# Attention and a two-layer MLP: split weight blocks of the first group stored in DRAM and read back by the second

## The chip, the cores and the metric

One core of a Trainium2 chip runs the whole program. The metric is the device time of one execution in microseconds; three executions of the kernel before gave 865.79, 866.02 and 866.52 us, a median of 866.02 us.

## The reference

Four batches, twelve heads, 448 positions, head size 64. The inputs q and k are scaled up (by 6.845 and 6.865), all is computed to float32 accuracy.

```python
scores = scale * np.matmul(q, k.transpose(0, 1, 3, 2))        # causal mask, softmax
attn_out = np.matmul(softmax(scores), v)                      # (4, 12, 448, 64)
x = attn_out.transpose(0, 2, 1, 3).reshape(4, 448, 768)
u = x + (x.transpose(0, 2, 1) @ U @ V).transpose(0, 2, 1)     # low rank mix of positions
out = u + np.maximum(u @ w_ch1, 0.0) @ w_ch2                  # 768 -> 3072 -> 768
```

The two weights w_ch1 and w_ch2 arrive as float64 words, which the kernel decodes to float32 itself.

## The kernel before

The matmuls of the MLP take their operands in a rounded form, fp32r. To keep float32 accuracy each operand is split into a high part (the value rounded, a cast) and a low part (value minus high part), and each product is made of three matmuls: high by high, high by low, low by high.

**First group.** After most of the attention (some 200 us of the profile; its remains are mixed in for a while) batches 0 and 1 go through the MLP in the ordinary way (`mlp`, L452). The weights come in 48 blocks of 128 x 768 values (`blocks`, L404): for each of eight steps p over the hidden width, three blocks of w_ch1 (columns of the hidden layer) and three of w_ch2. A block is loaded as words (`load_w`), decoded on ACT, DVE and POOL (`decode_w`, `decode_bit`, `decode_sum`), stored in DRAM as float32 (`kept`, L420) for the second group, and split into high and low parts in one of two slots of the SBUF tile `wsp`: the cast on ACT, the subtraction on DVE (`split`, L197; in its early pieces `weight_piece`). `decode_ahead` does this one to four blocks ahead of the one that TensorE is on: at the first quarter of block n the split of block n+1, at the second the decoding of n+2, at the fourth the store of n+2 and the load of n+4.

**Second group.** Batches 2 and 3 go through the same MLP by Strassen's method in Winograd's form (`strassen`, L871): a *quad* is a 2 x 2 arrangement of weight pieces t0, t1, t2, t3, and seven products take the place of eight. There are 12 quads of w_ch1 (kind 1, pieces of 128 x 384, 63 matmuls each) and 18 of w_ch2 (kind 2, pieces of 128 x 256, 42 matmuls each), 1512 matmuls in all. The seven weight operands of a quad are t0 and t1 (group "A1"), three sums of pieces (group "S": `S23` and `S1`), and t1 minus a sum, which is written over t2, and t3 (group "A2"). So t0, t1 and t3 are used as they are, t2 only in sums.

`load_quad` (L593) reads a quad's float32 pieces from `kept` into a ring in the tile `wld` (two DMAs for kind 1, L605; four for kind 2, L612). `prepare` (L622) then makes the high and low parts of each group in a ring in `wsp`: the cast on ACT (L634), the subtraction through the helper `adder` (L511) on the engine that `WE = "PVVP"` (L73) names, which is POOL for A1 and A2 and DVE for S. The sums are made on DVE in tiles `sw`. Nothing here has due times: at each product `strassen` issues the next load if its ring has room (`load_next`), up to two groups if theirs has (`prepare_next`), and one round of steps of each group in work (`emit`). Each engine, and the queue of SyncE (SP) that issues all DMAs, works in the order in which the program was written down, and waits in place.

The products accumulate in PSUM banks `sa`, `sb` and `se`. Between products that share a bank, DVE adds the bank to its place (`adder` into `xb` or `r`), or ACT copies it (L718) or applies the ReLU (L715) (`results`, L708). Between kind 1 and kind 2, `hidden` (L742) makes the split sums of the hidden layer (`h`, `tmp`): casts on ACT (L519) and subtractions on DVE (L511). In the last step p the results are stored from SP as they come (`stored`, L829). The helper's line L511 thus stands for many operations, and tiles tell them apart.

Of the kernel before, what the change touches and what calls it, by code (L numbers as in the profile page):

```python
# [10 lines left out]
F32 = mybir.dt.float32  # L11
# [4 lines left out]
ALU = mybir.AluOpType  # L16

B, H, S, D = 4, 12, 448, 64
DM, DFF, R = 768, 3072, 32
P = 128  # L20
# [3 lines left out]
NC = DM // P  # L24
FS = 8
FC = DFF // P // FS
WB = NC * P
# [45 lines left out]
WE = "PVVP"  # L73
# [5 lines left out]
def attention_mix_mlp(ctx: ExitStack, tc: tile.TileContext, qk, v, w1, w2, vu, out):  # L79
# [6 lines left out]
    nc = tc.nc  # L86

    def pool(name, bufs, **kw):
        return ctx.enter_context(tc.tile_pool(name=name, bufs=bufs, **kw))
# [3 lines left out]
    dram = pool("dram", 1, space=bass.MemoryType.DRAM)  # L93


    wsp = main.tile([P, WSP], F32R, tag="wsp", name="wsp")
# [31 lines left out]
    def f(ap):  # L128
        return ap.bitcast(F32)

    st = {}
# [24 lines left out]
    def decode_bit(t, n, piece, a=None):  # L156

        lo, hi = t[:, :n, 0], t[:, :n, 1]
        if piece == 0:
            st["nwa"] = st.get("nwa", -1) + 1  # L160
            a = main.tile([P, WB], U32, tag=f"wa{st['nwa'] % 2}", name="wa")[:, :n]
            nc.scalar.activation(f(a), f(hi), AF.Abs)
        elif piece == 1:
            nc.vector.tensor_scalar(f(a), f(a), HI_MIN, HI_MAX, op0=ALU.max, op1=ALU.min)
        elif piece == 2:
            nc.vector.tensor_scalar(a, a, 3, 0x3FFFFFF8, op0=ALU.logical_shift_left, op1=ALU.bitwise_and)
        elif piece == 3:
            nc.vector.scalar_tensor_tensor(hi, hi, 0xC0000000, a, op0=ALU.bitwise_and, op1=ALU.bitwise_or)  # L168
        else:
            nc.scalar.activation(lo.bitcast(I32), lo, AF.Copy, scale=2.0**-29)  # L170
        return a

    def decode_bits(t, n):
        a = None
        for piece in range(5):
            a = decode_bit(t, n, piece, a)
        return a

    def decode_sum(t, a, n):
        nc.gpsimd.tensor_tensor(  # L180
            a.bitcast(I32), t[:, :n, 1].bitcast(I32), t[:, :n, 0].bitcast(I32), op=ALU.add
        )
# [14 lines left out]
    def split(src, hi, lo):  # L197
        nc.scalar.copy(hi, src)  # L198
        nc.vector.tensor_tensor(lo, src, f(hi), op=ALU.subtract)  # L199
# [204 lines left out]
    blocks = []  # L404
    for p in range(FS):
        blocks += [w1[p, k] for k in range(FC)] + [w2[p, k] for k in range(NC // 2)]
    kept = [dram.tile([P, WB], F32, name=f"kept{n}") for n in range(len(blocks))]

    def load_w(n):
        if n < len(blocks):  # L410
            st["wr", n] = load_words(blocks[n], WB)

    def decode_w(n, step):
        if n >= len(blocks):
            return
        if step == 0:
            st["wa", n] = decode_bits(st["wr", n], WB)
        elif step == 1:
            decode_sum(st.pop(("wr", n)), st["wa", n], WB)
            nc.sync.dma_start(out=kept[n], in_=f(st["wa", n]))  # L420
        else:
            o = NC * 2 * S + n % 2 * 2 * WB
            wh, wl = wsp[:, o : o + WB], wsp[:, o + WB : o + 2 * WB]
            split(f(st.pop(("wa", n))), wh, wl)
            st["w", n] = wh, wl

    def weight_piece(n, piece):
        if piece == 0:
            load_w(n)
        elif piece < 6:  # L430
            st["wa", n] = decode_bit(st["wr", n], WB, piece - 1, st.get(("wa", n)))
        elif piece == 6:
            decode_w(n, 1)
        else:
            o = NC * 2 * S + n % 2 * 2 * WB
            wh, wl = wsp[:, o : o + WB], wsp[:, o + WB : o + 2 * WB]
            st["w", n] = wh, wl
            if piece == 7:
                nc.scalar.copy(wh, f(st["wa", n]))
            else:  # L440
                nc.vector.tensor_tensor(wl, f(st.pop(("wa", n))), f(wh), op=ALU.subtract)

    def decode_ahead(blk, quarter):
        if quarter == 0:
            decode_w(blk + 1, 2)
        elif quarter == 1:
            decode_w(blk + 2, 0)
        elif quarter == 3:
            decode_w(blk + 2, 1)
            load_w(blk + 4)  # L450
# [59 lines left out]
    def adder(o, a, b, op=ALU.add, e="V"):  # L510
        (nc.vector if e == "V" else nc.gpsimd).tensor_tensor(o, a, b, op=op)  # L511
# [48 lines left out]
    NQ = 2  # L560
# [29 lines left out]
    used = set()  # L590
# [31 lines left out]
    def prepare(q, group, at):  # L622

        kind, _, _ = q
        w = NC // 2 * P if kind == 1 else NQ * P
        t = st["t", q]

        for key, n in {"A1": (("A1", 2),), "S": (("S23", 2), ("S1", 1)), "A2": (("A2", 2),)}[group]:
            r = wsp[:, at : at + 2 * n * w].rearrange("p (l i w) -> p l i w", l=2, i=n)
            st["ws", q, key] = r[:, 0], r[:, 1]  # L630
            at += 2 * n * w

        def hi(key, src):
            return lambda: nc.scalar.copy(st["ws", q, key][0], src())  # L634

        def lo(key, e, src):
            def step():
                h, l = st["ws", q, key]
                adder(l, src(), f(h), ALU.subtract, e)
                used.add((q, key, "ready"))  # L640

            return step

        if group == "A1":
            return [[hi("A1", lambda: t[:, 0:2])], [lo("A1", WE[0], lambda: t[:, 0:2])]]
        if group == "A2":

            def end():
                used.add((q, "split"))

            return [[hi("A2", lambda: t[:, 2:4])], [lo("A2", WE[3], lambda: t[:, 2:4]), end]]
        s = {}

        def s13():
            st["sums"] = True
            s[0] = main.tile([P, WB], F32, tag="wa0", name="sw")[:, :w]
            s[1] = main.tile([P, WB], F32, tag="wa1", name="sw")[:, : 2 * w]
            s[1] = s[1].rearrange("p (i w) -> p i w", i=2)
            adder(s[0], t[:, 2], t[:, 3])
            adder(s[1][:, 1], t[:, 0], t[:, 2], ALU.subtract)  # L660

        def s2():
            adder(s[1][:, 0], s[0], t[:, 0], ALU.subtract)

        def s4():
            adder(t[:, 2], t[:, 1], s[1][:, 0], ALU.subtract)
            used.add((q, "s4"))

        return [
            [s13],  # L670
            [s2, s4],
            [hi("S23", lambda: s[1])],
            [hi("S1", lambda: s[0]), lo("S23", WE[1], lambda: s[1])],
            [lo("S1", WE[2], lambda: s[0]), lambda: st.pop("sums")],
        ]
# [7 lines left out]

    def product(q, n, ms):
        (key, i), j, bank = PRODUCTS[n]
        h, l = st["ws", q, key]
        steps = []
        for m in ms:
            if q[0] == 1:
                bh, bl = (u[:, j] for u in uc[m])  # L690
            else:
                bh, bl = st["H", q[1], m][j]
            cs = slice(m * P, (m + 1) * P)
            steps += [(h[:, i, cs], bh), (h[:, i, cs], bl), (l[:, i, cs], bh)]
        end = ms[-1] == (NC // 2 if q[0] == 1 else NQ) - 1
        for k, (a, b) in enumerate(steps):
            nc.tensor.matmul(  # L697
                st[bank, q], a, b,
                start=(n in FIRST and ms[0] == 0 and k == 0),
                stop=(n in LAST and end and k == len(steps) - 1),  # L700
                skip_group_check=True,
            )
# [137 lines left out]
    def prepare_next():  # L840

        if prepared[0] == len(units):
            return
        q, group = units[prepared[0]]
        if group == "A2" and (q, "s4") not in used:
            return
        if ("t", q) not in st or group == "S" and st.get("sums"):
            return
        w = NC // 2 * P if q[0] == 1 else NQ * P
        at = wsp_ring.take(2 * GROUPS[group] * w, (q, group))  # L850
        if at is None:
            return
        prepared[0] += 1
        prep.append(prepare(q, group, at))
# [54 lines left out]
    def attention():  # L909
# [12 lines left out]
        for of, at in EARLY.items():  # L922
            for piece, (n, slot) in enumerate(at):
                step = (low_rank_weights, (piece,)) if of == "vu" else (weight_piece, (of, piece))
                early.setdefault((n, slot), []).append(step)
# [24 lines left out]
    with tc.manual_schedule():  # L950
        constants()
        todo = attention()
        while todo[0][0] < len(pairs):
            _, step, a = todo.pop(0)
# [6 lines left out]
        for i, _ in enumerate(mlp()):  # L961
            while done < len(todo) and done * DRAIN < len(todo) * (i + 1):
                _, step, a = todo[done]
# [64 lines left out]
```

## Time and profile before

| | |
|---|---|
| median of three executions | 866.02 us |
| the profiled execution | 866.12 us, of which the span from first to last instruction 864.3 us |
| TensorE matmuls busy (PE) | 849.6 us (98%) |
| VectorE busy (DVE) | 687.5 us (80%) |
| ScalarE busy (ACT) | 461.2 us (53%) |
| GpSimd busy (POOL) | 309.4 us (36%) |
| DMA | 98.98 MB, 34.3% of the 16 engines' span |
| granted TensorE clock | 1.00 |

An engine's busy time is the union of its instructions' spans. Matmuls overlap: one over 448 columns is shown with some 366 ns, but the next starts sooner, so the busy share of TensorE hides short gaps, and its pace is read from the distance of starts. "[0.87 <-ACT r L718]" behind an instruction says that its engine sat idle for 0.87 us before it, and which instruction released it.

### The profile page before, as it was taken

The page shows a single profiled execution, that of the slowest core. Times are in us where ns is not written, and L with a number is a line of the kernel's source. Part 1 is how long each engine was busy: PE and PEld are TensorE (multiplying, and loading weights), DVE is VectorE, ACT ScalarE, POOL GpSimd, SP SyncE. Part 2 cuts the span into 40 slices and gives each one's busy share as a digit, 9 for nine tenths or more (in the row PEclk, how much of TensorE's full clock was granted, in tenths as well). Part 3 has the DMA queues.
Part 4 walks back from the last instruction along what each step waited for, and adds up shares of the span by engine and source line. Part 5 has one row for each costly group of instructions (what it writes and reads, how often), then busy time and mean ns, then how long its engine had stood idle before and what let it go on. Part 6 is the DMA issues. An engine that isn't in the chain of part 4 may idle for free.

```text
span 864.3 us, 13588 instructions
## 1 busy us (share of the span) xinstructions
PE 849.6 (98%) x4728; PEld 752.0 (87%) x4728; DVE 687.5 (80%) x1392; ACT 461.2 (53%) x978; POOL 309.4 (36%) x342
## 2 busy tenths in 40 slices
PE   7999999999999999999999999999999999999998
PEld 5777777789989999999999999889998998899886
DVE  6988888957667676767776768798998989898896
ACT  6998988854342444453445353463544635445520
POOL 4655777832212222213222323223333333333330
PEclk9999999999999999999999999999999999999999
DMA  6243343214344344444444457321121122212103
GB/s 206 98 147 119 112 134 97 69 60 158 122 161 149 125 165 165 165 165 165 165 165 165 165 165 264 96 60 50 43 80 49 61 61 61 70 41 74 38 1 128
DMA packets 47060, 98.98 MB, mean 115 GB/s; under 512 B 4240, under 2 KB 25744, under 8 KB 46992
## 3 DMA queue, kind: packets, MB, share of 16 engines
q1 hardware_dynamic: 46992, 98.12, 34.3%
q8 instruction: 37, 0.61, 0.3%
q14 instruction: 31, 0.25, 0.1%
HBM read 73.73 MB, written 24.38 MB: 114 GB/s over the span
## 4 chain that ended last, share of the span: by engine, by line
PE 87%; DVE 9%; ACT 2%; issue 2%; DMA 1%; DVEq 0%; ACTq 0%
PE hf L465 20%; PE of L490 20%; PE sa L697 15%; PE se L697 7%; PE s L244 6%; PE pv L313 6%; PE t L297 5%; PE sb L697 4%; DVE h L511 2%; DVE sw L511 2%; DVE tmp L511 1%; PE y L362 1%; PE xt L345 1%; DVE wsp L511 1%; DVE xb L511 1%
## 5 line engine op out<-in xcount | busy, mean ns | idle before, releaser
L511 POOL TENSOR_TENSOR wsp<-wld,wsp 128x512 fp32r<-128x512 f32 (+1 forms) x60 | 105.9, 1773 | 215.3 <-ACT wsp L634 127.6
L490 PE MATMUL of<-g,wsp 128*128 128x448 f32 x864 | 177.7, 366 | 0.0
L490 PEld LDWEIGHTS of<-g,wsp 128*128 128x128 f32 x864 | 162.1, 188 | 12.6
L180 POOL TENSOR_TENSOR wa<-wld 128x768 int32<-128x768 int32 (+1 forms) x49 | 73.0, 1489 | 261.9 <-DVE wld L168 190.9
L286 POOL TENSOR_SCALAR p<-p,r 112x112 f32<-112x112 f32 (+1 forms) x192 | 94.1, 507 | 61.6 <-DVE r L281 25.1
L273 ACT ACTIVATE p<-p,m 112x112 f32<-112x112 f32 x192 | 99.7, 525 | 13.6 <-DVE m L259 13.6
L198 ACT CAST wsp<-wa 128x768 fp32r<-128x768 f32 x47 | 39.3, 837 | 117.3 <-POOL wa L180 117.3
L697 PE MATMUL sa<-h,wsp 128*128 128x448 f32 x432 | 98.8, 368 | 1.9 <-DVE xb L511 1.9
L465 PE MATMUL hf<-wsp 128*128 128x448 f32 x432 | 92.8, 367 | 0.0
L465 PE MATMUL hf<-u,wsp 128*128 128x448 f32 x432 | 92.3, 366 | 0.0
L697 PE MATMUL sa<-uch,wsp 128*128 128x448 f32 x288 | 89.5, 371 | 2.8 <-ACT r L718 2.8
L259 DVE CUSTOM_DVE_ANT_0 p<-s,mask 112x112 f32<-112x112 f32 (+1 forms) x192 | 74.6, 442 | 20.9 <-PE s L244 19.4
L697 PEld LDWEIGHTS sa<-h,wsp 128*128 128x128 f32 x432 | 80.7, 188 | 10.7 <-DVE xb L511 3.8
L493 DVE TENSOR_TENSOR xa<-of,xa 128x448 f32<-128x448 f32 x96 | 59.3, 621 | 35.5 <-PE of L490 34.9
L465 PEld LDWEIGHTS hf<-u,wsp 128*128 128x128 f32 x432 | 81.0, 188 | 6.5
L465 PEld LDWEIGHTS hf<-wsp 128*128 128x128 f32 x432 | 80.8, 188 | 6.2
L199 DVE TENSOR_TENSOR wsp<-wa,wsp 128x768 fp32r<-128x768 f32 x47 | 50.9, 1084 | 22.8 <-ACT wsp L198 22.5
L473 ACT ACTIVATE g<-hf 128x448 fp32r<-128x448 f32 x48 | 26.1, 545 | 79.0 <-PE hf L465 79.0
L474 DVE SCALAR_TENSOR_TENSOR g<-hf,g 128x448 fp32r<-128x448 f32 x48 | 29.9, 624 | 43.7 <-ACT g L473 43.6
L634 ACT CAST wsp<-sw 128x256 fp32r<-128x256 f32 (+3 forms) x60 | 33.9, 575 | 56.6 <-DVE sw L511 25.7
L697 PEld LDWEIGHTS sa<-uch,wsp 128*128 128x128 f32 x288 | 54.1, 188 | 10.9 <-ACT r L718 6.0
L634 ACT CAST wsp<-wld 128x512 fp32r<-128x512 f32 (+1 forms) x60 | 41.8, 703 | 38.1 <-PE sa L697 28.6
(95 smaller groups left out, 1619.0 us busy)
## 6 DMA issues: line engine op xcount, KB each, us to landing
wld<-in_w_dram SPq DMA_DIRECT2D x48, 768.0 KB, 4.6
kept<-wa SPq DMA_DIRECT2D x48, 384.0 KB, 2.6
qk<-in_qk_dram SPq DMA_DIRECT2D x24, 448.0 KB, 3.8
wld<-kept SPq DMA_DIRECT2D x24, 384.0 KB, 3.2
wld<-kept SPq DMA_DIRECT2D x72, 128.0 KB, 2.4
v<-in_v_dram SPq DMA_DIRECT2D x24, 224.0 KB, 2.8
out_dram<-xa SPq DMA_DIRECT2D x12, 224.0 KB, 2.5
out_dram<-xb SPq DMA_DIRECT2D x12, 224.0 KB, 1.9
```

Source lines behind the costliest of these rows:

```text
L180: nc.gpsimd.tensor_tensor(a.bitcast(I32), t[:, :n, 1].bitcast(I32), t[:, :n, 0].bitcast(I32), op=ALU.add)
L244: nc.tensor.matmul(o, t[r, 0, i * CP : (i + 1) * CP], t[r, 1, :n], start=True, stop=True, skip_group_check=True,)
L259: nc.vector.tensor_tensor_reduce(out=st["p", b, h][:, POFF[i] : POFF[i] + n], in0=st.pop(("o", b, h, i)), in1=mask[:, S - n :], scale=-(D* ...
L273: nc.scalar.activation(pi, pi, AF.Exp, bias=m[:, i : i + 1], scale=-1.0, accum_out=l[:, i : i + 1])
L286: nc.gpsimd.tensor_scalar(pi, pi, r[:, i : i + 1], 1.0, op0=ALU.mult, op1=ALU.mult)
L313: nc.tensor.matmul(o[j * D : (j + 1) * D, kt * CP : S], v[:, kt, j, :], pt[:, n0 : n0 + S - kt * CP], start=j not in begun, stop=not left[ ...
L465: nc.tensor.matmul(o, a[:, cs], m, start=(kc + n == 0), stop=(kc + n == NC + 1))
L490: nc.tensor.matmul(o, a[:, cs], m, start=(fc + n == 0), stop=(fc + n == FC + 1))
L493: nc.vector.tensor_tensor(x, o, x, op=ALU.add)
L511: (nc.vector if e == "V" else nc.gpsimd).tensor_tensor(o, a, b, op=op)
L634: return lambda: nc.scalar.copy(st["ws", q, key][0], src())
L697: nc.tensor.matmul(st[bank, q], a, b, start=(n in FIRST and ms[0] == 0 and k == 0), stop=(n in LAST and end and k == len(steps) - 1), skip ...
```

## The change

The first group also stores the high and low parts of each block in DRAM (`kept_s`, by `keep_split`, from SP, right behind the split). It stores only what the second group uses: of a block of w_ch1 in the second half of the hidden width the second half of its columns, of a block of w_ch2 in the first half the even ones of its 128-column pieces, of all others everything. In the second group, group A1 becomes one step on SP that reads both pieces' parts into `wsp` (two DMAs for kind 1, four for kind 2), with no cast and no subtraction. Group A2 reads the parts of t3 (one DMA for kind 1, two for kind 2), and casts and subtracts only t2, on ACT and POOL as before. Group S, `load_quad` and the products stay.

```diff
+    kept_s = [dram.tile([P, 2, WB], F32, name=f"halves{n}") for n in range(len(blocks))]
+
+    def keep_split(n):
+        p, k = divmod(n, FC + NC // 2)
+        o = NC * 2 * S + n % 2 * 2 * WB
+        src = f(wsp[:, o : o + 2 * WB]).rearrange("p (l c) -> p l c", l=2)
+        dst = kept_s[n]
+        if k < FC and p >= FS // 2:
+            src, dst = src[:, :, WB // 2 :], dst[:, :, WB // 2 :]
+        elif k >= FC and p < FS // 2:
+            src, dst = (
+                t.rearrange("p l (f d c) -> p l f d c", d=2, c=P)[:, :, :, 0] for t in (src, dst)
+            )
+        nc.sync.dma_start(out=dst, in_=src)
...
             split(f(st.pop(("wa", n))), wh, wl)
             st["w", n] = wh, wl
+            keep_split(n)
...
                 nc.vector.tensor_tensor(wl, f(st.pop(("wa", n))), f(wh), op=ALU.subtract)
+                keep_split(n)
...
+        def kept_parts(key, i, j):
+            _, p, k = q
+            dst = st["ws", q, key][2][:, :, i]
+            if kind == 1:
+                n = p * NQ + k + j // 2 * DFF // P // 2
+                src = kept_s[n // FC * (FC + NC // 2) + n % FC]
+                nc.sync.dma_start(out=dst, in_=src[:, :, j % 2 * w : (j % 2 + 1) * w])
+                return
+            for m in range(NQ):
+                n = p * NQ + m + j % 2 * DFF // P // 2
+                src = kept_s[n // FC * (FC + NC // 2) + FC + k]
+                c = n % FC * 2 * P + j // 2 * P
+                nc.sync.dma_start(out=dst[:, :, m * P : (m + 1) * P], in_=src[:, :, c : c + P])
+
         if group == "A1":
-            return [[hi("A1", lambda: t[:, 0:2])], [lo("A1", WE[0], lambda: t[:, 0:2])]]
+
+            def load():
+                for i in range(2):
+                    kept_parts("A1", i, i)
+                used.add((q, "A1", "ready"))
+
+            return [[load]]
         if group == "A2":
-
-            def end():
+            part = lambda: t[:, 2]
+
+            def hi2():
+                kept_parts("A2", 1, 3)
+                nc.scalar.copy(st["ws", q, "A2"][0][:, 0], part())
+
+            def lo2():
+                h, l, _ = st["ws", q, "A2"]
+                adder(l[:, 0], part(), f(h[:, 0]), ALU.subtract, WE[3])
+                used.add((q, "A2", "ready"))
                 used.add((q, "split"))
 
-            return [[hi("A2", lambda: t[:, 2:4])], [lo("A2", WE[3], lambda: t[:, 2:4]), end]]
+            return [[hi2], [lo2]]
```

## Rows read from the trace of the kernel before

**Rows 1.** Busy time by stage: the first group's MLP, then the second group.
```profile
core 0: us, PE busy (x) PEld busy (x) DVE busy (x) ACT busy (x) POOL busy (x), PEclk, DMA share, GB/s
203.00:541.00 338.00, 338.00 (x1690) 312.60 (x1689) 240.38 (x344) 144.75 (x199) 87.62 (x56) 1.00 0.48 164
541.00:865.00 324.00, 314.13 (x1515) 282.60 (x1513) 282.77 (x423) 147.31 (x247) 100.08 (x58) 1.00 0.20 61
```

**Rows 2.** PE's waits in the second group: us in total, times, longest.
```profile
PE sa L697 <- ACT r L718: 2.8, 6, 0.9
PE sa L697 <- DVE xb L511: 1.9, 3, 0.9
PE sb L697 <- DVE xa L493: 0.6, 1, 0.6
PE se L697 <- DVE r L511: 0.2, 1, 0.2
```

**Rows 3.** Timeline of PE: first and last product of the second group (start, us).
```profile
541.38 0.37 PE L697 MATMUL sa<-uch,wsp 128*128 128x448 f32 x1
...
859.31 1.50 PE L697 MATMUL sa<-h,wsp 128*128 128x448 f32 x6 [0.72 <-DVE xb L511]
```

**Rows 4.** Chain that ended last, second group: one undisturbed piece (start, us, what).
```profile
615.59 5.54 PE sa L697 x27
```

**Rows 5.** POOL by form, second group: busy us, mean ns | idle before.
```profile
L511 POOL TENSOR_TENSOR wsp<-wld,wsp 128x512 fp32r<-128x512 f32 x36 | 56.3, 1572 | 110.7 <-ACT wsp L634 72.2 <-issue 9.6 <-DVE wsp L511 8.7
L511 POOL TENSOR_TENSOR wsp<-wld,wsp 128x768 fp32r<-128x768 f32 x22 | 46.0, 2094 | 97.1 <-ACT wsp L634 47.9 <-PE sa L697 14.2 <-PE sb L697 13.6
```

**Rows 6.** DVE by form, second group, three subtractions of the hidden layer.
```profile
L511 DVE TENSOR_TENSOR h<-tmp,h 128x896 fp32r<-128x896 f32 x24 | 33.7, 1406 | 3.4 <-ACT h L519 3.4
...
L511 DVE TENSOR_TENSOR tmp<-r,tmp 128x448 f32<-128x448 f32 x24 | 22.0, 916 | 0.5
...
L511 DVE TENSOR_TENSOR h<-r,h 128x448 fp32r<-128x448 f32 x12 | 11.9, 989 | 3.3 <-ACT h L519 3.2
```

**Rows 7.** Tile tmp in the second group: duration ns min/median/max.
```profile
L511 DVE TENSOR_TENSOR h<-tmp,h x24: 1073/1092/2750, 560.8 to 834.1; 128x896 fp32r<-128x896 f32 x24
L511 DVE TENSOR_TENSOR tmp<-r,tmp x24: 608/624/1739, 561.9 to 832.4; 128x448 f32<-128x448 f32 x24
```

**Rows 8.** Timeline around the longest stop, four engines.
```profile
720.47 0.47 PE L697 MATMUL sa<-uch,wsp 128*128 128x448 f32 x1 [0.87 <-ACT r L718]
...
718.95 0.62 ACT L634 CAST wsp<-wld 128x512 fp32r<-128x512 f32 x1
...
719.79 1.70 DVE L511 TENSOR_TENSOR h<-r,h 128x448 fp32r<-128x448 f32 x1
...
719.65 1.35 POOL L511 TENSOR_TENSOR wsp<-wld,wsp 128x512 fp32r<-128x512 f32 x1 [6.54 <-ACT wsp L634]
```

**Rows 9.** The page's slices: GB/s of DMA in 40 equal slices.
```profile
GB/s 206 98 147 119 112 134 97 69 60 158 122 161 149 125 165 165 165 165 165 165 165 165 165 165 264 96 60 50 43 80 49 61 61 61 70 41 74 38 1 128
```

**Rows 10.** The page's DMA issues: count, KB each, us to landing.
```profile
wld<-in_w_dram SPq DMA_DIRECT2D x48, 768.0 KB, 4.6
...
wld<-kept SPq DMA_DIRECT2D x24, 384.0 KB, 3.2
wld<-kept SPq DMA_DIRECT2D x72, 128.0 KB, 2.4
```

**Rows 11.** Line L612: time of one issue on SP, ns min/median/max.
```profile
L612 SPq DMA_DIRECT2D wld<-kept x72: 359/460/497, 536.0 to 807.0; - x72
```

**Rows 12.** SP's waits in the second group.
```profile
SPq L612 <- POOL wsp L511: 75.7, 14, 11.0
SPq L605 <- POOL wsp L511: 75.5, 13, 15.9
```

**Rows 13.** Timeline: two POOL subtractions and the PE pieces with their first use.
```profile
589.43 1.61 POOL L511 TENSOR_TENSOR wsp<-wld,wsp 128x512 fp32r<-128x512 f32 x1
...
598.11 0.57 PE L697 MATMUL sa<-h,wsp 128*128 128x448 f32 x2
...
769.94 2.81 POOL L511 TENSOR_TENSOR wsp<-wld,wsp 128x768 fp32r<-128x768 f32 x1 [3.78 <-PE sa L697]
...
777.09 0.79 PE L697 MATMUL sa<-uch,wsp 128*128 128x448 f32 x2
```

More of the change, by code (lines that the diff above doesn't have):

```diff
@@ L629, in prepare @@
             r = wsp[:, at : at + 2 * n * w].rearrange("p (l i w) -> p l i w", l=2, i=n)
-            st["ws", q, key] = r[:, 0], r[:, 1]
+            st["ws", q, key] = r[:, 0], r[:, 1], f(r)
             at += 2 * n * w
@@ L637, in step @@
             def step():
-                h, l = st["ws", q, key]
+                h, l, _ = st["ws", q, key]
                 adder(l, src(), f(h), ALU.subtract, e)
@@ L685, in product @@
         (key, i), j, bank = PRODUCTS[n]
-        h, l = st["ws", q, key]
+        h, l, _ = st["ws", q, key]
         steps = []
```

## The prediction

> **What bounds the kernel now.** I read the stages first [rows 1]. TensorE is the bound in both groups. In the first group's MLP it is busy for all 338.00 us, so nothing can be won there and the question is only what the new stores may cost. In the second group 314.13 of 324 us are busy, while DVE has 282.77 us of work, nearly as much; POOL and ACT have far less.
>
> Next the waits of PE in the second group [rows 2]: eleven, 5.5 us of idle time. None is for a weight. In each, PE stands before a PSUM bank that ACT (copy, L718) or DVE (add, L511 and L493) has not emptied yet. Idle time understates the loss, because a matmul is shown longer than the distance to the next. The full loss comes from the pace: an undisturbed piece does 27 matmuls in 5.54 us [rows 4], 0.2052 us each, so 1512 need 310.2 us. The stage takes 859.31 + 1.50 - 541.38 = 319.4 us [rows 3]. The stops thus cost 9.2 us. The last one, 0.72 us before 859.31 [rows 3], is the end of the dependence chain itself (two last products share a bank, nothing else is left to do); with the restart I put it at 1.0 us and leave it. So 8.2 us can go at most.
>
> Why are ACT and DVE late? The longest stop shows it [rows 8]. PE waits until 720.47 for an ACT copy. Among the casts that ACT did just in front of it is one of a group A1 (0.62 us). Beside it DVE runs a subtraction over 448 columns in 1.70 us, where the shortest of that size takes 0.608 us [rows 7]. A POOL subtraction, the low part of a weight group, started 0.14 us before it and ended at 721.00, and the DVE operation ended at 721.49: DVE stood still until POOL was through. This is no single case. Three kinds of subtraction of the hidden layer have means of 1406, 916 and 989 ns [rows 6] against shortest ones of 1073, 608 and 608 [rows 7]: 24 x 0.333 + 24 x 0.308 + 12 x 0.381 = 20.0 us of DVE time in the second group that is only standing beside POOL. The sums of weight pieces show the same and I leave them uncounted.
>
> **The change part by part.**
>
> *POOL in the second group.* 58 subtractions take 102.3 us there [rows 5] (two more run just before). The 30 of A1 go, the 30 of A2 halve: about 18 x 0.79 + 12 x 1.05 = 26.8 us stay, a quarter. With it a quarter of the 20.0 us of DVE's standing stays, 5 us, and 15 us leave DVE. POOL itself is on no path; its own gain is worth nothing.
>
> *ACT in the second group.* 30 casts go and 30 halve. A cast of A1 takes 0.62 us [rows 8] or somewhat more, and stands in front of the copies that PE waits for; some 25 to 30 us leave an engine with 147.31 us [rows 1].
>
> *What that gives PE.* Both engines that PE waits for get work taken out from just in front of the late operations. An average stop is 8.2/10 = 0.8 us; one clash that is avoided brings DVE forward by 1.70 - 0.61 = 1.1 us [rows 7, 8], and an avoided cast ACT by 0.6 us. So where a clash or cast stood before the stop, the stop goes whole. Bounds: none goes if DVE's own work is the cause (0), all go (-8.2 us). I take the share of POOL's work that disappears, three quarters, because the stretched operations stand near most of the stops: -6.1 us. What is late next is the last hidden layer, where DVE has a dense run of such subtractions with little POOL work beside it.
>
> *New loads in the second group.* 12 x 3 + 18 x 6 = 144 DMAs, 12 x 3 x 384 + 18 x 6 x 128 KB = 28.3 MB, over 319 us 89 GB/s more beside 61 [rows 1]. All are issued by SP, in order. An A1 load waits for its place in the ring (PE done with what lay there), as the cast did; behind it on SP queue the next `load_quad`, the other groups' loads and at the end the stores of the results. Before, from free place to ready took a cast and a subtraction, 0.62 + 1.57 = 2.2 us [rows 5, 8]. Now, for kind 2, four issues of 0.46 us [rows 11] and a landing of 2.4 us [rows 10]: 4.2 us; kind 1 two issues and 3.2 us, about the same. So the weights come 2 us later. Pairing the 60 POOL subtractions with the first product that uses each, in program order, the shortest distance of an A1 is 598.31 (the second matmul of the piece at 598.11) minus 591.04 = 7.3 us, the shortest of an A2 777.41 - 772.75 = 4.7 us [rows 13]; in that A2 the new load needs one issue and 3.2 us against the old subtraction's 2.81 us. The work that hides it is that distance, PE on the products before. Cost between 0 and, if a few of the tightest ones slip by 2 us each, 4 us; I take +0.5, since the rows lie nearer to the lower end.
>
> *New stores in the first group.* 48 stores, 24 of 768 KB and 24 of 384 KB, again 28.3 MB: 84 GB/s on top of 164 at a share of 0.48 [rows 1], so about 248 GB/s and a share of 0.73. The 25th slice already moves 264 GB/s [rows 9] inside the stretch in which PE never stops. A store waits on SP for DVE's low part; behind it stand the float32 store and the load of the words of a block that is decoded more than one block (7 us) later, against a landing of 4.6 us [rows 10]. The slot in `wsp` that a store reads is written again two blocks later, 14 us. Cost 0; if that cover were gone, one landing, 4.6 us, paid once and then carried along.
>
> No row shows compute beside DMA at a share of 0.73. The Trainium skill, "SBUF — State Buffer", section "Who interferes with whom", says that DMA never contends with a compute engine. By it the stores cost exactly 0, and the bound of 4.6 us falls away; the sum stays. [...]
>
> **Sum.** -6.1 + 0.5 + 0 = -5.6 us. The profiled execution took 866.12 us, 0.10 us over the median of 866.02. 866.02 - 5.6 = 860.4 us.
>
> **Rivals.**
>
> *All stops go (chance 0.17).* For it: DVE gets 15 us of slack plus what the weight sums gain, more than the 8.2 us lost. Against it: the densest stops lie in the last hidden layer, where DVE is full of its own work. Time 866.02 - 8.2 = 857.8 us.
>
> *DVE's own order is the cause (chance 0.13).* DVE has 282.77 us of work; without 15 us it is still the fullest engine after PE. If banks are emptied late because the operation stands behind others in the program's order, the stops shrink only by a fifth: -1.6 us, 864.4 us, or no change if the loads cost as much. Against it: the row at 719.79.
>
> *The weights come late (chance 0.10).* This one ends slower. SP waits 27 times for POOL, 151 us in all, up to 15.9 us at once [rows 12], and A1's loads now stand behind such a wait. If SP comes free after the ring's place, a `load_quad` goes first (four issues, 1.8 us), then 1.8 us of own issues and 2.4 us of landing: 6.1 us after SP is free, against 7.3 + 2.2 = 9.5 us from free place to first use. So the rival decides once SP is 3.4 us later than the place. Its break-even is 6.1/18 = 0.34 us of lateness for each of the 18 kind 2 quads; at 0.7 us each it costs 12.6 us and the time is 866.0 - 6.1 + 12.6 = 872.5 us. Against it: what SP waits for, A2's subtraction, becomes half as long, and stands earlier in the program than A1's place comes free.
>
> The Trainium skill, "DMA: Bandwidth & Descriptors", section "Latency and other measured facts", has an HBM access at 0.2 us on average and 2 us under high load. By an estimate from that page landings would rise by 1.8 us, and this rival would decide at 1.6 us instead of 3.4; no run here shows such a rise yet.
>
> **Chances.** The forecast (859 to 864.2 us) has 0.60, the rivals 0.17, 0.13 and 0.10. The measurement of this kernel tells no change from one within 0.2%, 1.7 us. Faster: 0.60 + 0.17, and a small part of the second rival, 0.78; same 0.13; slower 0.09. The range leaves out the slower rival and the upper part of the second, and reaches below the case in which all stops go: 857.2 to 865.5 us.
>
> **What would show it.** In the profile of the changed kernel: POOL's two groups of 128x512 and 128x768 replaced by 18 of 128x256 and 12 of 128x384; the mean of h<-tmp,h near 1.15 us instead of 1.41; PE's waits for ACT and DVE in the second group under 2 us; the stage from first to last product near 313.8 us instead of 319.4; the first group's 338 us unchanged with a DMA share near 0.73. It is wrong if PE waits for a DMA into `wsp` (third rival), if the DVE means fall and PE's waits stay (second), or if PE stops in the first group (the stores).

## The result and the profile after

The changed kernel took 857.43 us (median; 857.36 to 857.8), the kernel before 866.27 us beside it: a ratio of 0.9899 (95% interval 0.9882 to 0.9916), 8.8 us less. The prediction was 860.4 us, 5.6 us less. Sign and place were right; the gain was half as large again.

The stages of the changed kernel, in the columns of [rows 1]:

```profile
203.00:541.00 338.00, 338.00 (x1689) 312.31 (x1688) 239.17 (x346) 143.20 (x197) 82.91 (x54) 1.00 0.70 239
541.00:865.00 324.00, 310.32 (x1516) 283.62 (x1514) 249.22 (x421) 125.17 (x219) 29.29 (x29) 1.00 0.50 150
```

The first group is what it was: PE busy for all 338.00 us, with 239 instead of 164 GB/s beside it. In the second group POOL falls from 100.08 to 29.29 us, ACT by 22 us, and DVE by 33.6 us, though not one DVE instruction was taken out.

PE's waits, the whole list (us in total, times, longest):

```profile
PE s L244 <- DMA qk<-in_qk_dram: 4.4, 1, 4.4
PE t L297 <- POOL p L286: 1.9, 1, 1.9
PE sa L743 <- DVE xb L528: 0.8, 1, 0.8
PE s L244 <- DVE m L259: 0.2, 1, 0.2
```

Only the third is in the second group. Of the eleven stops of [rows 2] one is left, in front of the last product. PE's timeline, first and last product of the second group (start, us):

```profile
541.45 0.37 PE L743 MATMUL sa<-uch,wsp 128*128 128x448 f32 x1
...
850.66 1.47 PE L743 MATMUL sa<-h,wsp 128*128 128x448 f32 x6 [0.81 <-DVE xb L528]
```

From first start to last end that is 852.13 - 541.45 = 310.68 us, against 319.43 [rows 3]: 8.75 us, the whole gain. DVE's three subtractions, to be read beside [rows 6], and POOL's two forms, beside [rows 5] (busy us, mean ns | idle before):

```profile
L528 DVE TENSOR_TENSOR h<-tmp,h 128x896 fp32r<-128x896 f32 x24 | 27.2, 1132 | 2.4 <-ACT h L536 2.4
L528 DVE TENSOR_TENSOR tmp<-r,tmp 128x448 f32<-128x448 f32 x24 | 14.9, 621 | 0.5
L528 DVE TENSOR_TENSOR h<-r,h 128x448 fp32r<-128x448 f32 x12 | 8.4, 699 | 4.6 <-ACT h L536 4.6
```

```profile
L528 POOL TENSOR_TENSOR wsp<-wld,wsp 128x256 fp32r<-128x256 f32 x18 | 16.5, 914 | 111.0 <-ACT wsp L689 62.2 <-PE se L743 18.4 <-ACT r L761 13.4
L528 POOL TENSOR_TENSOR wsp<-wld,wsp 128x384 fp32r<-128x384 f32 x11 | 12.9, 1174 | 160.7 <-ACT wsp L689 99.9 <-issue 32.9 <-PE se L743 17.1
```

The means fell from 1406, 916 and 989 ns to 1132, 621 and 699, close to the shortest ones of [rows 7]. The change did three things at once, though: it took work from POOL, work from ACT, and added DMA. Which of them gave the 8.75 us was left to the runs.

### The profile page after: what moved, and what is told of

Its sections match the earlier page's. It is cut to its first block, busy times and chain, and to the rows that moved or that the text cites. A ratio compares the mean times of both kernels' runs of the same rounds, so it can differ in the third digit from the quotient of the medians.

```text
span 855.6 us, 13903 instructions
## 1 busy us (share of the span) xinstructions
PE 844.8 (99%) x4728; PEld 752.0 (88%) x4728; DVE 652.3 (76%) x1392; ACT 437.8 (51%) x948; POOL 234.4 (27%) x312
## 4 chain that ended last, share of the span: by engine, by line
PE 98%; DVE 1%; DMA 0%; ACT 0%; issue 0%
PE sa L743 21%; PE hf L482 21%; PE of L507 20%; PE se L743 10%; PE s L244 6%; PE pv L313 6%; PE t L297 6%; PE sb L743 5%; PE y L362 1%; PE xt L345 1%; PE hm L380 1%; PE hm L381 1%; DMA qk<-in_qk_dram 0%; DVE p L259 0%; ACT p L273 0%; DVE xb L528 0%
## 5 line engine op out<-in xcount | busy, mean ns | idle before, releaser
L528 POOL TENSOR_TENSOR wsp<-wld,wsp 128x256 fp32r<-128x256 f32 (+1 forms) x30 | 30.3, 1013 | 281.2 <-ACT wsp L689 171.6
L651 ACT CAST wsp<-sw 128x256 fp32r<-128x256 f32 (+3 forms) x60 | 34.2, 579 | 80.6 <-PE sa L743 31.8
L244 PE MATMUL s<-qk 64*112 64x448 f32 (+3 forms) x384 | 54.7, 422 | 4.6 <-DMA qk<-in_qk_dram 4.4
```

The lines of the kernel that those rows point to most:

```text
L244: nc.tensor.matmul(o, t[r, 0, i * CP : (i + 1) * CP], t[r, 1, :n], start=True, stop=True, skip_group_check=True,)
```

## The experiments

Ratios are to the kernel before on the same chip, with 95% intervals. Second-group figures are for 541 us to the end. Of each edit the main lines are shown.

**ACT or POOL?** Two kernels load one half each. *low_loaded* loads the low parts, and ACT casts every high part as before the change. *high_loaded* loads the high parts, and POOL makes every low part as before.

```diff
 low_loaded, in kept_parts and the steps of A1, A2
-dst = st["ws", q, key][2][:, :, i]
+dst = st["ws", q, key][2][:, 1:2, i]     # src likewise
+nc.scalar.copy(st["ws", q, "A1"][0], t[:, 0:2])
+nc.scalar.copy(st["ws", q, "A2"][0], t[:, 2:4])   # instead of t2 alone
 high_loaded
+dst = st["ws", q, key][2][:, 0:1, i]     # src likewise
+return [[load], [lo("A1", WE[0], lambda: t[:, 0:2])]]
+adder(l, t[:, 2:4], f(h), ALU.subtract, WE[3])
```

> The second group loads only the low parts of t0, t1 and t3; ACT casts all highs as before the change, so POOL loses its 30 A1 subtractions and half of each A2 one, and ACT loses nothing. Theory (POOL beside DVE made DVE late): as the whole change, 857 to 859 us, PE's waits under 2 us, mean of h<-tmp,h near 1.13 us. Rival (ACT's casts in front of the PSUM copies were the cause): the stops come back, 863 to 866 us.

> The other half alone: the high parts of t0, t1 and t3 are loaded, ACT casts only t2, and POOL makes all its subtractions at full size as before the change. Theory (POOL beside DVE): most of the gain is gone, 863 to 866 us, mean of h<-tmp,h near 1.4 us, PE waits 4 to 6 us. Rival (ACT's casts): 857 to 859 us.

low_loaded took 857.75 us, ratio 0.99 [0.9886, 0.9915]; high_loaded 871.92 us, 1.0064 [1.0049, 1.0079]. Their second groups in the columns of [rows 1], low_loaded first, then PE's waits there:

```profile
541.00:875.00 334.00, 310.42 (x1515) 283.49 (x1513) 248.42 (x422) 148.73 (x247) 28.58 (x29) 1.00 0.35 102
```

```profile
PE sa L745 <- DVE xb L529: 0.7, 1, 0.7
```

high_loaded, the same two views:

```profile
541.00:875.00 334.00, 315.81 (x1514) 281.68 (x1513) 288.43 (x421) 122.81 (x219) 102.33 (x60) 1.00 0.35 102
```

```profile
PE sa L743 <- ACT r L764: 5.9, 6, 1.5
PE sa L743 <- DVE xb L529: 2.8, 4, 1.5
PE se L743 <- DVE xb L529: 0.6, 1, 0.6
PE sa L743 <- POOL wsp L529: 0.3, 1, 0.3
```

With ACT at 148.73 us (147.31 before) and POOL relieved the whole gain is there, and no wait for ACT. With ACT relieved and POOL at 102.33 us (100.08 before) there is none; PE still waits for ACT, 5.9 us. So "<- ACT" in [rows 2] named the last link: the cause lay in POOL.

An edit can also change the order in which an engine's operations stand. In low_loaded it did not: by their records in the second group, ACT, DVE and PE do the same operations in the same order as in the kernel before. high_loaded has the changed kernel's order on these three. That it is 5.5 us *slower* than the kernel before, beyond the 863 to 866 us expected, fits only in part (DVE's standing grew, table below); the rest is open.

**Is it POOL's reading beside DVE?** Three kernels put work back into the changed one, into a scratch tile that nothing reads: the A1 subtraction on POOL (*pool_reads*), the A1 cast on ACT (*act_casts*), and three POOL memsets for each quad, which only write (*pool_writes*).

```diff
+scr = main.tile([P, 768], F32, tag="scr", name="scr")
 pool_reads, in load()
+adder(o, t[:, 0:2], f(h), ALU.subtract, "P")      # o: a view of scr
 act_casts
+nc.scalar.copy(scr_view, t[:, 0:2])
 pool_writes
+for _ in range(3):
+    nc.gpsimd.memset(scr[:, : 2 * w], 0.0)
```

> The changed kernel, and POOL makes the 30 subtractions of A1 again, of the same size from the same operands, into a scratch tile that nobody reads. Two thirds of the POOL work that the change took out are back (51 of 77 us), no cast, and nothing waits for the result. Theory (POOL beside DVE): about two thirds of the gain are lost, 861 to 865 us, with DVE's means up again. Rival (ACT's casts, or the place in the order): 857 to 858 us, since ACT and the weights are as in the changed kernel.

> The changed kernel, and ACT makes the 30 casts of A1 again, of the same size, into a scratch tile that nobody reads. They do not wait for a place in the ring, only take ACT's time (some 21 us). Theory (POOL beside DVE): 857 to 858.5 us. Rival (ACT's time in front of the copies): 861 to 865 us.

> The changed kernel, and in place of the dropped subtraction of each A1 POOL fills a scratch tile three times (memset, 128x768 or 128x512, no input read): some 60 us of POOL time in the second group, about as much as in the run in which POOL subtracted into a scratch tile (49 us more). Theory, sharp form (POOL's reads beside DVE's two-input operations are what stretches them): 857 to 858 us, h<-tmp,h near 1.13 us. Blunt form (any POOL work on SBUF beside DVE): 861 to 865 us as with the subtractions.

pool_reads took 862.71 us, 0.9953 [0.9935, 0.9971]: 50.8 of the 70.8 us of POOL's work that had gone came back (72%), and 5.3 of the 8.8 us were lost again (60%; by the ratios 53%). Its five executions lie between 859.53 and 864.22 us, so the loss is known as about half and no closer. DVE, ACT and PE have the changed kernel's order. Its second group and the waits of PE there:

```profile
541.00:875.00 334.00, 313.01 (x1514) 282.36 (x1512) 271.98 (x420) 123.57 (x219) 80.09 (x59) 0.99 0.49 144
```

```profile
PE sa L747 <- DVE xb L529: 1.7, 4, 0.8
PE sa L747 <- ACT r L768: 1.7, 3, 1.3
```

DVE grew by 22.8 us without one more instruction, and waits for ACT are back, with ACT at 123.57 us.

act_casts took 861.26 us, 0.9939 [0.9922, 0.9956], which looks like a price for ACT's casts. The timeline (ACT) and low_loaded say otherwise:

```profile
803.95 0.62 ACT L682 COPY scr<-wld 128x512 f32<-128x512 f32 x1 [1.64 <-DMA wld<-kept]
...
807.68 0.62 ACT L682 COPY scr<-wld 128x512 f32<-128x512 f32 x1 [2.68 <-DMA wld<-kept]
...
809.80 0.53 ACT L766 COPY r<-sa 128x448 f32<-128x448 f32 x1
```

A cast into the scratch waits for no place in the ring, so ACT can come to it before its weights have landed: it waited 2.68 us for them, with the copy that PE needed behind it. Across the second group ACT stood 31.8 us for such landings; in the kernel before no cast of ACT waited for one. The run tested a wait that I had put in together with ACT's time; it decides nothing between the two.

pool_writes took 860.91 us, 0.9932 [0.9915, 0.9949], 3.5 us above the changed kernel, with DVE, ACT and PE in the same order. All 90 memsets ran between 528 and 593 us, so that stretch is the test, here for pool_writes and then for the changed kernel:

```profile
541.00:593.00 52.00, 52.00 (x254) 47.29 (x253) 42.49 (x71) 25.00 (x45) 48.03 (x78) 1.00 0.58 182
```

```profile
541.00:593.00 52.00, 52.00 (x255) 47.43 (x254) 41.80 (x71) 25.20 (x46) 5.05 (x5) 1.00 0.65 200
```

POOL was busy 48.03 instead of 5.05 us, 44.4 of it with memsets; DVE's 71 instructions took 42.49 instead of 41.80 us, and PE never stopped. By the timelines, 44 DVE operations with both inputs in SBUF ran beside memsets alone, and none took over 10 ns more than the median of its form in dve_subs (below), where POOL is silent. POOL that only writes leaves DVE alone. The Trainium skill, "SBUF — State Buffer", section "Who interferes with whom", says just this: a DVE instruction with two SBUF inputs contends with a GpSimd instruction that reads SBUF, not with one that only writes. Both runs agree.

The profiled execution took 862.43 us, 5.0 us more than that of the changed kernel, and most of this was lost at one place, behind the memsets: the prediction's third rival, seen at work. SP's wait in 575:600, then the timelines of SP and PE:

```profile
SPq L630 <- POOL wsp L529: 5.6, 1, 5.6
```

```profile
591.52 0.87 SPq L630 DMA_DIRECT2D wld<-kept  x2
592.49 4.01 SPq L675 DMA_DIRECT2D wsp<-halves  x5
...
597.61 1.00 PE L746 MATMUL se<-h,wsp 128*128 128x448 f32 x3 [2.29 <-DMA wsp<-halves]
```

POOL came late to a subtraction, the `load_quad` that waits for it held SP for 5.6 us, the loads into `wsp` stood behind it, and PE waited 2.29 us for one of them. Then the granted clock of 597:602 was 0.66, a mixture of the two levels (2.4 and 1.2 GHz), before it was 1.00 again:

```profile
597.00:602.00 5.00, 4.39 (x14) 3.94 (x15) 1.74 (x3) 0.00 (x0) 0.00 (x0) 0.66 0.87 218
```

By my estimate the low clock cost 5.00 x (1 - 0.66) = 1.7 us, with the stop 4.0 of the 5.0 us.

**What do the DMAs cost?** *stores_only* adds just the stores to the kernel before. *twice_issued* splits each of the changed kernel's loads in two, so 288 issues instead of 144. *a1_loaded* loads A1 alone and makes A2 as before.

```diff
 stores_only, on the kernel before: in the first group's decoder
+keep_split(n)
 twice_issued
+for h in (slice(0, 64), slice(64, P)):
+    nc.sync.dma_start(out=dst[h], in_=src[h])     # columns as before
 a1_loaded, A2
+return [[hi("A2", lambda: t[:, 2:4])], [lo("A2", WE[3], lambda: t[:, 2:4]), end]]
```

> The kernel before with the 48 stores of the first group added and nothing else; what they store is not read. Prediction's term: 0 us, so 866 to 866.8 us, first group's stretch 338 us busy at a DMA share near 0.7. Rival (stores delay the words or hold DVE or PE): 868 us or more.

> The changed kernel with each of the 144 new loads issued as two DMAs over 64 partitions: SP issues 144 more, some 66 us more of its time, for the same bytes. Tests the cover that the slower rival disputes. If the loads are far ahead: 857 to 858 us. If the cover is nearly used up: 859 to 865 us, with PE or DVE waiting for DMAs.

> The changed kernel with the parts of t3 made again in the second group: A1 is loaded, A2 has its cast and its POOL subtraction at full size as before the change. POOL has half its subtractions. If the stops follow the standing of DVE beside POOL: DVE busy near 266 us in the second group, half of the gain or somewhat more, 859 to 863 us. If any halving of POOL's work is enough: 857 to 858.5 us.

stores_only took 866.32 us, 1.0 [0.9991, 1.001]: 28 MB of stores under the first group cost nothing that can be measured. Its first group:

```profile
203.00:541.00 338.00, 338.00 (x1689) 312.30 (x1688) 240.38 (x344) 144.71 (x199) 87.36 (x56) 1.00 0.70 240
```

twice_issued took 857.4 us, 0.9902 [0.9888, 0.9917]: twice the issues for the same bytes, no change, and PE waits for none of them. a1_loaded took 858.83 us, 0.992 [0.9905, 0.9935], between the two ranges that I had expected:

```profile
541.00:875.00 334.00, 311.00 (x1512) 282.80 (x1511) 259.12 (x421) 130.85 (x219) 50.48 (x29) 0.99 0.38 116
```

A1, half of POOL's work, gives 6.9 us by its ratio, and takes more from DVE than I had reckoned (259.12 us instead of 266). Its interval and that of the changed kernel overlap, so the rest that A2 adds is small, but not resolved.

**Without DMA at all: the same work elsewhere or shorter.** On the kernel before, *dve_subs* gives the subtractions to DVE itself, and *split_subs* cuts each POOL subtraction in two.

```diff
 dve_subs
-WE = "PVVP"
+WE = "VVVV"
 split_subs, in lo.step
+for i in range(2):
+    adder(l[:, i], src()[:, i], f(h[:, i]), ALU.subtract, e)
```

> The kernel before with the 60 subtractions of A1 and A2 moved from POOL to DVE. POOL is idle in the second group, so no DVE operation is stretched, but DVE gets 36 x 0.69 + 24 x 0.95 = 48 us of work for the 42 us of standing that go. Theory in the form 'DVE's occupied time is what counts': 866 to 872 us, PE's waits as before or more. Form 'being stretched at the wrong moment is what counts': 858 to 862 us.

> The kernel before with each of POOL's 60 subtractions made as two of half the width, one after the other, so the same POOL work in pieces of some 0.65 to 0.95 us. Theory 'a DVE operation stands until the POOL instruction beside it ends, and the length of one standing is what makes the drains late': standings of at most about 1 us, fewer stops, 859 to 864 us. Rival 'the amount of POOL time beside DVE counts': as before the change, 865.5 to 868 us.

dve_subs took 858.89 us, 0.9913 [0.9898, 0.9928]: one line, no DMA, and 7.4 of the 8.8 us. Its second group, the waits of PE there, and its tile tmp, to be read beside [rows 7]:

```profile
541.00:875.00 334.00, 310.45 (x1515) 283.31 (x1513) 281.29 (x480) 149.08 (x247) 0.00 (x0) 0.99 0.20 59
```

```profile
PE sa L697 <- DVE xb L511: 1.9, 2, 1.2
```

```profile
L511 DVE TENSOR_TENSOR h<-tmp,h x24: 1081/1085/1093, 558.9 to 825.6; 128x896 fp32r<-128x896 f32 x24
L511 DVE TENSOR_TENSOR tmp<-r,tmp x24: 615/618/621, 560.5 to 823.2; 128x448 f32<-128x448 f32 x24
```

DVE is as busy as before (281.29 against 282.77 us), ACT too, and the stops are nearly gone. Min and max now lie 12 and 6 ns apart, where they were 1677 and 1131: with POOL silent there is no standing at all.

This edit did move operations: by the records of the second group 23 of ACT's 247 and 54 of PE's 1513 (nearly all after 817 us), and many of DVE's, stand elsewhere than before. So dve_subs does not tell the silence of POOL from the new order. low_loaded, pool_reads and split_subs do.

split_subs took 863.46 us, 0.9975 [0.9965, 0.9986], with DVE, ACT and PE in the order of the kernel before. POOL's time *rose* to 122.99 us, and yet the kernel became a little faster, as the longest h<-tmp,h fell from 2750 to 1899 ns:

```profile
L511 DVE TENSOR_TENSOR h<-tmp,h x24: 1075/1130/1899, 559.4 to 831.3; 128x896 fp32r<-128x896 f32 x24
```

**The last stop.** One stop is left in the changed kernel, two products that share a PSUM bank at the very end. *end_order* exchanges two entries of the written order in the last quad of the kernel; *dve_subs_end* does so on dve_subs.

```diff
-order((k3, 0), (k3, 3), (k1, 5), (k3, 2), (k3, 1), (k3, 6), (k3, 4))
+tail = ((k3, 6), (k3, 4)) if p + 1 < NPART else ((k3, 4), (k3, 6))
+order((k3, 0), (k3, 3), (k1, 5), (k3, 2), (k3, 1), *tail)
```

> The changed kernel with the last two products but one exchanged: product 6 (bank e) stands between the products 4 and 5 that share bank a, so the last product need not wait for DVE to empty the bank. Expected: the last stop of PE (0.81 us idle, some 1.0 us with the restart) goes, 856.2 to 856.6 us. Rival (the end is set by the adds and the stores, not by PE): 857.2 to 857.6 us.

> The kernel before with two small edits and no new DMA: POOL's 60 subtractions on DVE, and products 6 and 4 of the last quad exchanged. Expected from the two alone: 858.9 - 0.8 = 858.1 us; it would beat the changed kernel only if the remaining stop of 1.2 us before the last hidden layer went too (856.9 us).

end_order took 856.67 us, 0.9888 [0.9873, 0.9903], the fastest kernel of the study. PE's waits, all of them:

```profile
PE s L244 <- DMA qk<-in_qk_dram: 4.0, 1, 4.0
PE t L297 <- POOL p L286: 2.1, 1, 2.1
PE s L244 <- DVE m L259: 0.2, 1, 0.2
```

None is in the second group. Against the changed kernel that is 0.8 us, the length of the stop; the two intervals overlap, so the row shows it better than the times. dve_subs_end took 858.04 us, 0.9911 [0.9895, 0.9928]. PE's stop at the end is gone there too, but the ratio cannot be told from dve_subs's 0.9913, nor from the changed kernel's 0.9899, whose 56 MB of traffic it does without.

**Together.** "Standing" is worked out from the timelines: over all DVE additions and subtractions after 541 us, the duration less the median of the same form in dve_subs, counted above 60 ns. The kernel before took 865.5 to 866.4 us on the chips used, so the ratio stands beside the time.

| kernel | POOL us | DVE us | standing us (times) | PE waits us | time us | ratio |
|---|---|---|---|---|---|---|
| high_loaded | 102.33 | 288.43 | 46.6 (47) | 9.6 | 871.9 | 1.0064 |
| before | 100.08 | 282.77 | 39.9 (46) | 5.5 | 866.3 | 1 |
| split_subs | 122.99 | 275.18 | 32.4 (66) | 3.9 | 863.5 | 0.9975 |
| pool_reads | 80.09 | 271.98 | 30.5 (41) | 3.4 | 862.7 | 0.9953 |
| a1_loaded | 50.48 | 259.12 | 16.1 (19) | 1.4 | 858.8 | 0.992 |
| dve_subs | 0 | 281.29 | 0 | 1.9 | 858.9 | 0.9913 |
| low_loaded | 28.58 | 248.42 | 3.6 (10) | 0.7 | 857.8 | 0.99 |
| after | 29.29 | 249.22 | 4.9 (11) | 0.8 | 857.4 | 0.9899 |

The time goes with the standing, though not in proportion to it (a1_loaded), and not with how busy DVE (dve_subs) or ACT (low_loaded) is.

## Why the prediction came out as it did

**Where the time is lost: right.** PE's stops in the second group before banks emptied late, 8.2 us of them removable: the stage shrank by 8.75 us. The bound was small because the undisturbed pace is a little quicker than the one piece that I took it from: with 1.0 us again left for the end, (310.68 - 1.0) / 1512 = 0.2048 us, 0.6 us less over the stage.

**Why banks were late: half right.** DVE standing beside POOL is the cause, shown by low_loaded, high_loaded and pool_reads. ACT's casts, which I made the second cause (an avoided cast brings ACT forward by 0.6 us), are none: low_loaded keeps them all. My reading of [rows 8] was wrong as well. The subtraction that stands there ended at 721.49 us, 1.02 us after PE had gone on, so it did not hold up that copy. An earlier one did, in the kernel before:

```profile
711.85 1.67 DVE L511 TENSOR_TENSOR wld<-wld,sw 128x384 f32<-128x384 f32 x1
...
716.41 0.94 ACT L519 CAST h<-tmp 128x896 fp32r<-128x896 f32 x1 [2.99 <-DVE tmp L511]
```

This operation takes 0.55 us in dve_subs and took 1.67. From it DVE ran on without a pause to the result for which ACT had waited 2.99 us, and ACT ran on without a pause to the copy. The timelines show the same before all six stops for ACT: its last wait of over 1 us was for DVE (1.5 to 3.0 us), and DVE had come to that result without a pause from an operation that stood for 0.57 to 1.67 us. So ACT hands DVE's lateness on to PE. Its longest sum of waits for DVE, in the kernel before and, with the same order, in low_loaded:

```profile
ACT r L715 <- DVE r L511: 35.2, 24, 3.2
```

```profile
ACT r L763 <- DVE r L529: 15.8, 20, 1.9
```

**The mis-sized term: three quarters of the stops.** I let the stops go in the proportion in which POOL's work goes, -6.1 us. All went: the first rival, to which I gave 0.17. The forecast itself (859 to 864.2 us) missed; the measured time lies in my range only because the range was drawn down to 857.2 us to take that rival in. Standing did not fall in that proportion either: from 39.9 to 4.9 us, 88%, with POOL's work at 29%. What stays on POOL is in shorter pieces (914 and 1174 ns instead of 1572 and 2094), and split_subs shows that shorter pieces harm less even where their sum is larger. My 20.0 us was also too small a sum: I counted three forms and left out the weight sums, which stand too. Of the missing 3.2 us, this term is 2.1, the pace 0.6, and the loads 0.5.

**Loads, +0.5 us: 0.** PE waits for no DMA into `wsp` in the changed kernel, and for none with twice the issues. In the changed kernel DVE waited for one once (2.4 us) and POOL three times (7.9 us), at no cost that PE's waits show. The changed kernel's page, DMA issues in the columns of [rows 10]:

```profile
wsp<-halves SPq DMA_DIRECT2D x36, 384.0 KB, 4.0
wsp<-halves SPq DMA_DIRECT2D x108, 128.0 KB, 2.7
```

Landings took longer than I had set (3.2 and 2.4 us), and the distances covered it. The shortest from the issue of a unit's last load to its first product was 6.4 us, at the first unit, where landings took longest: its two loads landed at 540.46 and 541.54 us, 6.9 and 6.5 us after their issue, and the products of the two pieces, paired in the order of the program, began at 541.45 and 543.30 us. About 1 us of cover was left there.

**Stores, 0: right**, at a DMA share of 0.70 where I had 0.73. The bound of 4.6 us was for a landing that comes late, which is a wait and not contention; stores_only shows no such wait.

**Second rival (DVE's own order): fell.** It held that DVE without 15 us would still be the fullest engine and so late. low_loaded has the order of the kernel before on DVE, ACT and PE, and nearly no stops. dve_subs has DVE full and nearly no stops, so an engine's sum of work was the wrong quantity. What is not shown is why 45.6 us of subtractions of its own, placed by the program's order, do so much less harm than 39.9 us of standing. That they come as pieces of at most about 1 us at places that the order knows is argued only; the changed order of that run is another possible reason.

**Third rival (weights late): did not happen, but is real.** Its conditions did not arise, since SP's waits for POOL fell from 151 [rows 12] to 24 us (the changed kernel, 535 to 860 us); pool_writes made them arise, and the chain ran as described in its main steps.

```profile
SPq L629 <- POOL wsp L528: 14.0, 8, 4.4
SPq L622 <- POOL wsp L528: 10.2, 6, 3.7
```

**"Late next: the last hidden layer": wrong for this change**, where only the stop at the very end is left; dve_subs has a stop of 1.2 us there, at 827.90 us.

## What to carry to other kernels

Compare shortest, median and longest duration of one form of instruction: where they differed here, DVE stood beside POOL, and the wait that PE showed named only the last link. Before a POOL instruction with two SBUF inputs is replaced by traffic through DRAM, try it on the engine that it disturbs: one line gave 7.4 of the 8.8 us. Count what a queue's waiting head holds up: one late POOL instruction became a PE stop of 2.3 us by way of SP.

## What the hardware showed that was not expected

- Only a DVE operation that began second stood. In all 46 cases in the kernel before, a POOL subtraction had begun before the DVE operation, and the DVE operation ended after it: at [rows 8] 0.49 us after, having taken 1.70 us instead of 0.61. Nine more began second and did not stand; of 22 with both inputs in SBUF that began first, none did (overlaps over 0.1 us). With memsets on POOL for 44 of 52 us there was nothing of the kind.
- Only DVE operations with both inputs in SBUF stood. Of its additions from a PSUM bank 51 ran beside a POOL subtraction in the kernel before, and none took over 10 ns more than the median of its form in dve_subs.
- PE at 338.00 of 338 us beside DMA at a share of 0.70 and 240 GB/s, no different from 0.48 and 164 GB/s.
- After PE had stood for 2.29 us the granted clock of the next 5 us was 0.66; in high_loaded, with stops of up to 1.5 us, the second group's mean stayed at 1.00.
